# Weight decoding in a fused attention and mixture kernel: the sign bit taken on GpSimd for 18 of 32 half slices

## The chip, the cores and the metric

One core of a Trainium2 chip runs the whole program once. The metric is the device time of one execution in microseconds (us). The engines are named as the profile names them: PE (TensorE matmul) and PEld (its weight loads), DVE (VectorE), ACT (ScalarE), POOL (GpSimd), SP (SyncE, which issues most of the DMAs).

## What is computed

Three layers follow each other on 3072 tokens of 512 features.

```python
attn_out = _attn_ref(**attn_kwargs)        # chunked attention, 4 batches x 8 heads x 768 x 64, with 8 memory keys
x = attn_out.transpose(0, 2, 1, 3).reshape(B * S, H * D)
h = x @ w_in                               # 3072x512 @ 512x2048
g = h * (1.0 / (1.0 + np.exp(-h)))
x = (g @ w_out).astype(np.float32)         # 3072x2048 @ 2048x512
...                                        # then a gate, an assignment of 384 tokens to each of 8 experts,
h = np.maximum(x[mask] @ w1[e], 0.0)       # and two matmuls per expert
out[mask] = h @ w2[e]
```

`w_in` and `w_out` of the second layer arrive as 64-bit floats. The kernel has to make 32-bit floats of them on the chip, and this decoding is what the change is about.

## The kernel before

The tokens go in 8 batches of 384 (`NB`, `TB`). For each batch the second layer's hidden dimension is cut into 16 slices of 128 (`NF`). A pass of the main loop is one slice `f` of one batch `n`: `gemm1(n, f)` makes the hidden values on PE (L298), `swish` turns them into `gh` and `gl` (a tanh on ACT at L307, a product on DVE at L309, a rounded copy on ACT at L316, the rest on POOL at L317), and `gemm2` of two passes before adds its product to the accumulators (L334). Every 32-bit operand is split in a rounded part and a remainder, so that three matmuls make one exact enough product. The attention of the next batch is threaded through the passes in four items (pairs of heads): scores (`att_s`, L200 on PE, L205 on DVE, L211 on ACT), normalizing (`att_n`, L220 and L221 on DVE, L222 on POOL), transposes (`att_t`, L230 on PE, L241 on ACT) and the product with the values (`att_av`, `att_x`).

The weights of a slice are decoded once, in the opening and the passes of the first batch, and stay in SBUF. There are 32 items, one for the half of `w_in` and one for the half of `w_out` of each slice. An item is a tile `w` of 128 x 512 pairs of words (512 KB) and goes through four stages, one stage per tick:

- `w_load` (L136): SP issues the DMA. There are five buffers, so a load waits until POOL has finished with the item five before it.
- `w_bias` (L146): ACT reads the high words as floats and scales them into a PSUM bank, which moves the exponent to where a 32-bit float has it.
- `w_bits`: three DVE operations on 128 x 512 words. L152 shifts by 3, L153 ors in the upper bits of the low word, L155 ors in the sign, which it masks out of the high word.
- `w_split`: ACT rounds the result (L162), POOL subtracts the rounded part (L163).

`tick` calls the stages last first, so that one tick holds the split of item j, the bits of item j+1, the bias of item j+2 and a load. The opening is a hand-written order of steps (`PRO`, where `w0` to `w3` are the four stages; five items have their bias there). Each pass of the first batch has two ticks: `tick("a2")` ahead of `gemm1`, `tick("a1")` between `gemm1` and `gemm2`. Each engine takes its instructions in the order in which this Python code issues them; nothing reorders them later.

In the first batch `swish` is called at the end of the pass (`finish()`), so on DVE a pass reads: bits of tick a2, bits of tick a1, the product L309. On ACT it reads: the rounding copy and bias of tick a2, those of tick a1, tanh, and, as soon as DVE has L309, the copy `gh`. On POOL: the subtract of tick a2, that of tick a1, `gl`. The passes are called 0 to 15 below. The four attention items have their scores in passes 0, 3, 7 and 11, the normalizing one pass later, the transposes two passes later, the product with the values three passes later.

Of the kernel before, what the change touches and what calls it, by code (L numbers as in the profile page):

```python
# [13 lines left out]
OP = mybir.AluOpType  # L14
# [34 lines left out]
def body(ctx, tc, qk_in, v_in, wcat1, wcat2, wgt, consts, masks, iconst, bconst, out):  # L49
    nc = tc.nc  # L50
    PE, V, A, G, S = nc.tensor, nc.vector, nc.scalar, nc.gpsimd, nc.sync
# [12 lines left out]
    def bank(tag):  # L64
        return ps.tile([128, 512], F32, tag=tag, name=tag)
# [64 lines left out]
    wstage = {}  # L130
# [7 lines left out]
        wstage[i] = t  # L138

    whigh = {}  # L140

    def w_bias(i, tag):

        high = wstage[i][:, :, 1].bitcast(F32)
        whigh[i] = bank(tag)
        A.activation(out=whigh[i], in_=high, func=AF.Copy, scale=2.0 ** -112)  # L146

    def w_bits(i, tag):

        low, high = wstage[i][:, :, 0], wstage[i][:, :, 1]  # L150
        x = whigh.pop(i).bitcast(I32)
        V.tensor_scalar(out=x, in0=x, scalar1=3, scalar2=None, op0=OP.logical_shift_left)  # L152
        V.scalar_tensor_tensor(out=x, in0=low, scalar=29, in1=x,  # L153
                               op0=OP.logical_shift_right, op1=OP.bitwise_or)
        V.scalar_tensor_tensor(out=low, in0=high, scalar=-2147483648, in1=x,  # L155
                               op0=OP.bitwise_and, op1=OP.bitwise_or)
# [9 lines left out]
    def advance(k, tag="a2"):  # L166

        if stage[k] < len(items) and (k == 0 or stage[k] < stage[k - 1]):
            (w_load, w_bias, w_bits, w_split)[k](stage[k], tag)
            stage[k] += 1  # L170

    def tick(tag):
        for k in (3, 2, 1, 0):
            if k != 1 or stage[0] > stage[1] + 1 or stage[0] == len(items):
                advance(k, tag)
# [316 lines left out]
    for op in PRO.split():  # L492
        c, i, e = op[0], int(op[1]), (S, A)[op[2:] == "a"]
# [56 lines left out]
    for g in range((NB - 1) * NF):  # L550
# [8 lines left out]

        attend(0)  # L560
        tick("a2")
        finish = gemm1(n, f)
        if n > 0:
            finish()
        attend(1)
        tick("a1")
        if g >= 2:
            m, k = divmod(g - 2, NF)
# [678 lines left out]
```

## Time and profile before

| | us |
|---|---|
| median of 3 runs (lowest, highest) | 1001.63 (1001.45, 1002.49) |
| the profiled execution | 1001.23 |
| its span | 999.1 |
| PE busy | 964.9 (97%) |
| DVE busy | 682.4 (68%) |
| POOL busy | 423.3 (42%) |
| ACT busy | 404.5 (40%) |
| mean granted TensorE clock | 0.984 |

The busy shares are means over the whole span. In the 40 slices of the page PE stands at 9 tenths from the third slice on and at 7 in the first two (25 us each), while DVE has 6, 8, 8, 8, 5 in the first five. The decoding (L146 to L163) lies between 13 us and 112 us. The profiled execution lasts 1001.23 us, of which 999.1 are its span; 2.1 us lie around it.

### The profile page before, as it was taken

How to read it: one execution, taken by the hardware profiler on the slowest of the kernel's cores; microseconds unless marked ns; L12 is line 12 of the kernel's file. 1: busy time of each engine (PE TensorE's matmuls, PEld its weight loads, DVE VectorE, ACT ScalarE, POOL GpSimd, SP SyncE). 2: the span in 40 equal slices, each digit the busy share in tenths (PEclk: the TensorE clock that was granted, in tenths of full speed). 3: DMA queues.
4: the chain of work that ended last, by engine and by line, in shares of the span. 5: the costliest groups of instructions: out<-in, count | busy, mean ns of one | idle time of the engine just before them, and what ended most of it. 6: DMA issues, size and time to landing. Idle time of an engine off the chain costs nothing.

```text
span 999.1 us, 19120 instructions
## 1 busy us (share of the span) xinstructions
PE 964.9 (97%) x7193; PEld 841.0 (84%) x7193; DVE 682.4 (68%) x1958; ACT 404.5 (40%) x1000; POOL 423.3 (42%) x335
## 2 busy tenths in 40 slices
PE   7799999999999999999999999999999989999997
PEld 5687788988898888988888997778888878899996
DVE  6888578988898998898248664666766757632110
ACT  7677544343444344344343440023433333443441
POOL 3566523323232332232222441146555554767761
PEclk8799999999999999999999999999999989999999
DMA  8667321111112111111021500325444442555420
GB/s 287 214 216 231 107 81 58 39 64 41 56 64 65 32 65 60 37 64 64 33 96 45 171 1 2 127 86 189 133 143 126 129 148 85 169 169 166 151 74 31
DMA packets 34061, 102.86 MB, mean 103 GB/s; under 512 B 4145, under 2 KB 7857, under 8 KB 33970
## 3 DMA queue, kind: packets, MB, share of 16 engines
q1 hardware_dynamic: 29698, 88.63, 27.8%
q0 software_dynamic: 3840, 12.59, 3.9%
q8 instruction: 56, 0.92, 0.4%
q10 hardware_dynamic: 432, 0.43, 0.2%
q14 instruction: 35, 0.29, 0.1%
HBM read 86.69 MB, written 14.94 MB: 102 GB/s over the span
## 4 chain that ended last, share of the span: by engine, by line
PE 81%; DVE 8%; issue 3%; ACT 2%; DMA 2%; another core or an unknown queue 1%; POOL 1%; SPq 0%; POOLq 0%; DVEq 0%; ACTq 0%
PE acc L334 24%; PE h L298 23%; PE h L1045 12%; PE acc L1072 11%; PE a L772 3%; PE a L256 2%; PE a L230 2%; DVE a L153 2%; PE a L200 2%; DVE a L152 2%; DVE w L155 1%; DMA w<-in_wcat 1%; DVE junk L423 1%; PE a L971 1%
## 5 line engine op out<-in xcount | busy, mean ns | idle before, releaser
L298 PE MATMUL h<-xh,big 128*128 128x384 f32 x1024 | 289.4, 343 | 1.6 <-DVE th L309 1.6
L317 POOL TENSOR_TENSOR gl<-th,gh 128x384 fp32r<-128x384 f32 x112 | 123.3, 1101 | 253.6 <-ACT gh L316 249.7
L334 PE MATMUL acc<-big,gh 128*128 128x512 f32 x636 | 202.5, 399 | 1.2 <-ACT w L393 1.2
L298 PEld LDWEIGHTS h<-xh,big 128*128 128x128 f32 x1024 | 189.7, 190 | 9.8 <-DVE th L309 2.6
L1018 POOL TENSOR_TENSOR big<-w,big 128x1024 fp32r<-128x1024 f32 x64 | 152.4, 2394 | 71.7 <-ACT big L1017 69.1
L298 PE MATMUL h<-xl,big 128*128 128x384 f32 x512 | 174.5, 341 | 0.2 <-DVE xl L276 0.2
L334 PEld LDWEIGHTS acc<-big,gh 128*128 128x128 f32 x636 | 115.4, 189 | 21.9 <-ACT w L393 1.6
L1072 PE MATMUL acc<-big,gh 128*128 128x512 f32 x384 | 125.1, 402 | 0.0
L334 PE MATMUL acc<-big,gl 128*128 128x512 f32 x318 | 124.7, 392 | 0.0
L1045 PE MATMUL h<-xh,big 128*128 128x384 f32 x512 | 116.9, 344 | 0.7 <-ACT xh L987 0.7
L307 ACT ACTIVATE th<-h 128x384 f32<-128x384 f32 x128 | 62.3, 487 | 133.7 <-PE h L298 130.4
L423 DVE SCALAR_TENSOR_TENSOR junk<-wg_sum,w 128x512 bf16<-128x512 f32 x128 | 112.7, 880 | 3.3
L309 DVE SCALAR_TENSOR_TENSOR th<-th,h 128x384 f32<-128x384 f32 x128 | 69.8, 545 | 65.5 <-ACT th L307 65.4
L316 ACT ACTIVATE gh<-th 128x384 fp32r<-128x384 f32 x112 | 58.8, 525 | 126.5 <-DVE th L309 126.5
L298 PEld LDWEIGHTS h<-xl,big 128*128 128x128 f32 x512 | 97.6, 191 | 4.1 <-DVE xl L276 0.7
L1049 ACT ACTIVATE gh<-h 128x384 fp32r<-128x384 f32 x64 | 31.4, 491 | 160.8 <-PE h L1045 145.4
L1045 PEld LDWEIGHTS h<-xh,big 128*128 128x128 f32 x512 | 91.5, 189 | 5.8 <-ACT xh L987 0.9
L412 DVE SCALAR_TENSOR_TENSOR junk<-w 128x512 bf16<-128x512 f32 x96 | 86.2, 898 | 2.3
L1054 DVE SCALAR_TENSOR_TENSOR gl<-h,gh 128x384 fp32r<-128x384 f32 x64 | 35.4, 552 | 73.9 <-ACT gh L1049 73.8
L1072 PEld LDWEIGHTS acc<-big,gh 128*128 128x128 f32 x384 | 71.0, 190 | 8.9
L1072 PE MATMUL acc<-big,gl 128*128 128x512 f32 x192 | 77.1, 401 | 0.0
L211 ACT ACTIVATE s<-s,m 128x96 f32<-128x96 f32 x168 | 60.8, 364 | 26.8 <-DVE m L205 26.8
(216 smaller groups left out, 1446.6 us busy)
## 6 DMA issues: line engine op xcount, KB each, us to landing
w<-in_wcat SPq DMA_DIRECT2D x96, 512.0 KB, 3.8
qk<-in_qk_in SPq DMA_DIRECT2D x28, 480.0 KB, 4.4
v<-in_v_in SPq DMA_DIRECT2D x28, 288.0 KB, 3.0
x2d<-w SPq DMA_DIRECT2D x16, 256.0 KB, 2.0
w<-in_wgt SPq DMA_DIRECT2D x4, 512.0 KB, 6.4
x2d<-x SPq DMA_DIRECT2D x8, 256.0 KB, 2.1
back<-gd SPq DMA_DIRECT2D x2, 768.0 KB, 6.1
big<-in_qk_in SPq DMA_DIRECT2D x3, 480.0 KB, 7.4
```

Source lines behind the costliest of these rows:

```text
L211: A.activation(out=s[:, b, :], in_=s[:, b, :], func=AF.Exp, scale=-1.0, bias=m[:, b:b + 1], accum_out=m[:, 6 + b:7 + b])
L298: PE.matmul(b[:, :TB], w1[:, o:o + 128], (xh, xl, xh)[p][:, c, :], start=not done, stop=len(done) == 11)
L307: A.activation(out=th, in_=b[:, :TB], func=AF.Tanh, scale=0.5)
L309: V.scalar_tensor_tensor(out=u, in0=th, scalar=1.0, in1=b[:, :TB], op0=OP.add, op1=OP.mult)
L316: A.activation(out=gh, in_=u, func=AF.Copy)
L317: G.tensor_tensor(out=gl, in0=u, in1=gh.bitcast(F32), op=OP.subtract)
L334: PE.matmul(a, g[:, 128 * t:128 * t + 128], w2[:, o:o + 512], start=(f in first and p == 0), stop=(f + 1 in (*first, NF) and p == 2))
L412: V.scalar_tensor_tensor(out=junk, in0=xs[k], scalar=1.0, in1=late["w"][e], op0=OP.mult, op1=OP.mult, accum_out=Lg[:, k, e:e + 1])
L423: V.scalar_tensor_tensor(out=junk, in0=t, scalar=0.5, in1=late["w"][e], op0=OP.mult, op1=OP.mult, accum_out=part2[:, f % 4, e:e + 1])
L1018: G.tensor_tensor(out=l, in0=t, in1=h.bitcast(F32), op=OP.subtract)
L1045: PE.matmul(b[:, :TB], (h, h, l)[p][:, 128 * c:128 * c + 128], (xh, xl, xh)[p][:, c, :], start=(p == 0 and c == 0), stop=(p == 2 and c == 3))
L1072: PE.matmul(a, (gh, gh, gl)[p][:, 128 * t:128 * t + 128], (h, l, h)[p][:, 512:1024], start=(s % 8 == 0 and p == 0), stop=(s % 8 == 7 and p ...
```

## The change

For some items POOL makes the sign bit from the high words, in place, as a part of the bias stage: `(high < 0) * -2**31`, written as an integer, is the sign bit alone. The bits stage of such an item is then two DVE operations: shift the biased word and or in the sign, then or in the low word's upper bits. Which items: those whose bias is in the opening, and in the loop those whose bias is in `tick("a1")`. These are 5 and 13, 18 of 32; the other 14 keep three DVE operations.

```diff
     whigh = {}
+    part_signs = [True]
+
+
+    parted = {}
 
     def w_bias(i, tag):
 
         high = wstage[i][:, :, 1].bitcast(F32)
         whigh[i] = bank(tag)
         A.activation(out=whigh[i], in_=high, func=AF.Copy, scale=2.0 ** -112)
+        if parted.setdefault(i, part_signs[0]):
+
+            G.tensor_scalar(out=wstage[i][:, :, 1], in0=high, scalar1=0.0, scalar2=-2.0 ** 31, op0=OP.is_lt, op1=OP.mult)
 
     def w_bits(i, tag):
 
         low, high = wstage[i][:, :, 0], wstage[i][:, :, 1]
         x = whigh.pop(i).bitcast(I32)
+        if parted[i]:
+            V.scalar_tensor_tensor(out=x, in0=x, scalar=3, in1=high, op0=OP.logical_shift_left, op1=OP.bitwise_or)
+            V.scalar_tensor_tensor(out=low, in0=low, scalar=29, in1=x,
+                                   op0=OP.logical_shift_right, op1=OP.bitwise_or)
+            return
         V.tensor_scalar(out=x, in0=x, scalar1=3, scalar2=None, op0=OP.logical_shift_left)
...
     def tick(tag):
+        part_signs[0] = tag == "a1"
         for k in (3, 2, 1, 0):
```

The order of PE, ACT and SP does not change. An item whose bias is in tick a1 of a pass has its bits in tick a2 of the next pass, so in each pass the first decode on DVE is the shorter one.

On POOL, passes 3 to 5 (from `gl` of pass 3 to `gl` of pass 5; `s` is the normalizing of an attention item, the L163 rows are the splits of ticks a2 and a1). Before:

```order
L317 TENSOR_TENSOR gl<-th,gh 128x384 [waits PE_49,Activation_49]
L163 TENSOR_TENSOR big<-w,big 128x512 [waits DMAHW2_49,Activation_49]
L222 TENSOR_TENSOR s<-s,m 128x576 [waits DVE_49]
L163 TENSOR_TENSOR big<-w,big 128x512 [waits DMAHW3_49,Activation_49]
L317 TENSOR_TENSOR gl<-th,gh 128x384 [waits PE_49,Activation_49]
L163 TENSOR_TENSOR big<-w,big 128x512 [waits DMAHW4_49,Activation_49]
L163 TENSOR_TENSOR big<-w,big 128x512 [waits DMAHW5_49,Activation_49]
L317 TENSOR_TENSOR gl<-th,gh 128x384 [waits PE_49,Activation_49]
```

With the change (L153 is the sign, L175 the split, L235 the normalizing, L330 `gl`):

```order
L330 TENSOR_TENSOR gl<-th,gh 128x384 [waits PE_49,Activation_49]
L175 TENSOR_TENSOR big<-w,big 128x512 [waits DMAHW2_49,Activation_49]
L235 TENSOR_TENSOR s<-s,m 128x576 [waits DVE_49]
L175 TENSOR_TENSOR big<-w,big 128x512 [waits Activation_49]
L153 TENSOR_SCALAR w<-w 128x512 [waits DMAHW5_49,Activation_49,Pool_49]
L330 TENSOR_TENSOR gl<-th,gh 128x384 [waits PE_49,Activation_49]
L175 TENSOR_TENSOR big<-w,big 128x512 [waits DMAHW4_49,Activation_49]
L175 TENSOR_TENSOR big<-w,big 128x512 [waits Activation_49]
L153 TENSOR_SCALAR w<-w 128x512 [waits DMAHW1_49,Activation_49,Pool_49]
L330 TENSOR_TENSOR gl<-th,gh 128x384 [waits PE_49,Activation_49]
```

The sign stands behind both subtracts of its pass (and behind the normalizing where there is one) and ahead of `gl`.

On DVE, from the product of pass 3 to that of pass 4 (`th`), with the normalizing between the two decodes. Before:

```order
L309 SCALAR_TENSOR_TENSOR th<-th,h_592 128x384 [waits Activation_49]
L152 TENSOR_SCALAR a_626<-a_626 128x512
L153 SCALAR_TENSOR_TENSOR a_626<-w,a_626 128x512 [waits DMAHW3_49,DVE_49]
L155 SCALAR_TENSOR_TENSOR w<-w,a_626 128x512 [waits DVE_49,Pool_49]
L220 TENSOR_SCALAR m<-m 128x6
L221 RECIPROCAL m<-m 128x6 [waits DVE_49]
L152 TENSOR_SCALAR a_686<-a_686 128x512 [waits Activation_49]
L153 SCALAR_TENSOR_TENSOR a_686<-w,a_686 128x512 [waits DMAHW4_49,DVE_49]
L155 SCALAR_TENSOR_TENSOR w<-w,a_686 128x512 [waits DVE_49,Pool_49]
L309 SCALAR_TENSOR_TENSOR th<-th,h_690 128x384 [waits Activation_49]
```

With the change:

```order
L322 SCALAR_TENSOR_TENSOR th<-th,h_592 128x384 [waits Activation_49]
L160 SCALAR_TENSOR_TENSOR a_626<-a_626,w 128x512 [waits DMAHW3_49,Pool_49]
L161 SCALAR_TENSOR_TENSOR w<-w,a_626 128x512 [waits DVE_49]
L233 TENSOR_SCALAR m<-m 128x6
L234 RECIPROCAL m<-m 128x6 [waits DVE_49]
L164 TENSOR_SCALAR a_686<-a_686 128x512 [waits Activation_49]
L165 SCALAR_TENSOR_TENSOR a_686<-w,a_686 128x512 [waits DMAHW4_49,DVE_49]
L167 SCALAR_TENSOR_TENSOR w<-w,a_686 128x512 [waits DVE_49]
L322 SCALAR_TENSOR_TENSOR th<-th,h_690 128x384 [waits Activation_49]
```

The first decode's opening row waited for nothing new and now waits for POOL's sign; one row is gone.

On POOL at the end of the opening, with the change (before there are the four L163 rows alone):

```order
L175 TENSOR_TENSOR big<-w,big 128x512 [waits Activation_49]
L153 TENSOR_SCALAR w<-w 128x512 [waits DMAHW7_49,Activation_49]
L175 TENSOR_TENSOR big<-w,big 128x512 [waits Activation_49]
L153 TENSOR_SCALAR w<-w 128x512 [waits DMAHW1_49,Activation_49]
L175 TENSOR_TENSOR big<-w,big 128x512 [waits Activation_49]
```

These are the split of item 1, the sign of item 3, the split of item 2, the sign of item 4, the split of item 3.

## Rows read from the trace of the kernel before

**Rows 1.** Busy time by engine, 80 to 90 us (`PE, PEld, DVE, ACT, POOL`, clock, DMA share, GB/s).
```profile
80.00:90.00 10.00, 9.07 (x66) 7.64 (x67) 9.34 (x16) 7.27 (x15) 8.13 (x8) 1.00 0.58 204
```
**Rows 2.** Chain of waits, 0 to 120 us, shares by line.
```profile
by line: DVE a L153 13.0%; DVE a L152 12.5%; DVE w L155 9.7%; DMA w<-in_wcat 9.4%; issue 9.1%; DMA big<-in_qk_in 6.2%; PE h L298 5.5%; ACT s L211 4.9%; PE acc L334 4.2%; DVE th L309 2.9%; DVE m L220 2.8%; ACT a L146 2.7%; ACT big L162 2.3%;
```
**Rows 3.** Waits of PE, 28 to 110 us (us in total, times, longest).
```profile
PE a L230 <- POOL s L222: 3.4, 3, 1.6
PE a L230 <- ACT at L241: 1.9, 3, 0.8
```
**Rows 4.** The three decode operations (ns: shortest, median, longest).
```profile
L152 DVE TENSOR_SCALAR a<-a x30: 673/693/699, 14.0 to 106.3; 128x512 int32<-128x512 int32 x30
L153 DVE SCALAR_TENSOR_TENSOR a<-w,a x30: 695/697/697, 14.7 to 107.0; 128x512 int32<-128x512 int32 x30
L155 DVE SCALAR_TENSOR_TENSOR w<-w,a x30: 689/689/692, 15.4 to 107.8; 128x512 int32<-128x512 int32 x30
```
**Rows 5.** Timeline of DVE, passes 3 to 11 (start us, us, instruction).
```profile
52.24 0.55 DVE L309 SCALAR_TENSOR_TENSOR th<-th,h 128x384 f32<-128x384 f32 x1 [1.26 <-ACT th L307]
58.02 0.55 DVE L309 SCALAR_TENSOR_TENSOR th<-th,h 128x384 f32<-128x384 f32 x1
58.48 0.69 DVE L152 TENSOR_SCALAR a<-a 128x512 int32<-128x512 int32 x1
59.21 0.69 DVE L153 SCALAR_TENSOR_TENSOR a<-w,a 128x512 int32<-128x512 int32 x1
60.61 0.69 DVE L152 TENSOR_SCALAR a<-a 128x512 int32<-128x512 int32 x1
62.75 0.55 DVE L309 SCALAR_TENSOR_TENSOR th<-th,h 128x384 f32<-128x384 f32 x1
67.95 0.55 DVE L309 SCALAR_TENSOR_TENSOR th<-th,h 128x384 f32<-128x384 f32 x1
75.10 0.55 DVE L309 SCALAR_TENSOR_TENSOR th<-th,h 128x384 f32<-128x384 f32 x1 [1.27 <-ACT th L307]
97.97 0.55 DVE L309 SCALAR_TENSOR_TENSOR th<-th,h 128x384 f32<-128x384 f32 x1 [1.28 <-ACT th L307]
```
**Rows 6.** Timeline of ACT behind the product of pass 4.
```profile
58.60 0.53 ACT L316 ACTIVATE gh<-th 128x384 fp32r<-128x384 f32 x1 [2.03 <-DVE th L309]
59.03 0.65 ACT L162 ACTIVATE big<-w 128x512 fp32r<-128x512 f32 x1
59.58 0.62 ACT L146 ACTIVATE a<-w 128x512 f32<-128x512 f32 x1
```
**Rows 7.** Timeline of POOL, passes 3 to 5.
```profile
53.43 1.02 POOL L317 TENSOR_TENSOR gl<-th,gh 128x384 fp32r<-128x384 f32 x1 [4.42 <-ACT gh L316]
54.41 1.32 POOL L163 TENSOR_TENSOR big<-w,big 128x512 fp32r<-128x512 f32 x1
56.07 1.15 POOL L222 TENSOR_TENSOR s<-s,m 128x576 f32<-128x576 f32 x1 [0.34 <-DVE m L221]
57.18 1.31 POOL L163 TENSOR_TENSOR big<-w,big 128x512 fp32r<-128x512 f32 x1
60.19 2.63 POOL L163 TENSOR_TENSOR big<-w,big 128x512 fp32r<-128x512 f32 x2
```
**Rows 8.** Groups of POOL by shape (busy us, mean ns, idle before).
```profile
L163 POOL TENSOR_TENSOR big<-w,big 128x512 fp32r<-128x512 f32 x32 | 42.0, 1312 | 12.3 <-ACT big L162 12.2
L1018 POOL TENSOR_TENSOR big<-w,big 128x1024 fp32r<-128x1024 f32 x64 | 152.4, 2394 | 71.7 <-ACT big L1017 69.1 <-DVE ind L763 2.3
```
**Rows 9.** Timeline of the end of the opening: splits, bias and bits of items 1 and 4.
```profile
21.54 1.31 POOL L163 TENSOR_TENSOR big<-w,big 128x512 fp32r<-128x512 f32 x1 [2.12 <-ACT big L162]
23.80 0.64 ACT L146 ACTIVATE a<-w 128x512 f32<-128x512 f32 x1 [0.61 <-DMA w<-in_wcat]
25.63 0.69 DVE L152 TENSOR_SCALAR a<-a 128x512 int32<-128x512 int32 x1
```
**Rows 10.** Waits of ACT for loads, 0 to 120 us.
```profile
ACT a L146 <- DMA w<-in_wcat: 1.3, 2, 0.7
```

## Prediction

> **What bounds the kernel now.** I read the busy time by stretches first, to see whether one stage differs from the rest. It does: from 80 to 90 us DVE is busy 9.34 of 10 us, PE 9.07 and POOL 8.13 [rows 1], while the whole program is 97% PE. So a saving on DVE counts in the stage in which the weights are decoded and nowhere else. The chain of waits says the same: of the first 120 us, 35% lie on the three decode lines [rows 2]. The waits of PE show where it pays for that: at the transposes, which wait for POOL's normalizing and for ACT's copy of the first half [rows 3], both of which hang on DVE. Behind pass 13 PE stands at 9 tenths or more in nearly every slice of the page and has no such waits, so the gain of the whole program is how much earlier pass 13's transposes come.
>
> The timeline of DVE gives the clock of this stage: the products (L309) of passes 3 to 7 start at 52.24, 58.02, 62.75, 67.95 and 75.10 us, and that of pass 11 at 97.97 [rows 5]. So four passes, with one attention item in them, take 22.86 us, twice in a row (22.87 the second time). The single passes take 5.78, 4.73, 5.20 and 7.15.
>
> **What is removed.** One decode occupies DVE for 60.61 - 58.48 = 2.13 us; its first operation takes 59.21 - 58.48 = 0.73 of that [rows 5]. The new pair is two operations of the kind of L153 and L155, with one operand in SBUF and one in PSUM as those have, 696 and 690 ns [rows 4], so it takes the other 1.40. 18 items save 18 x 0.73 = 13.1 us of DVE time. This would be the gain if nothing else came in. Two things do.
>
> **ACT behind the first decode.** The second decode of a pass needs the bias of tick a2. After a product at t, ACT starts `gh` at t + 0.58, the rounding copy at t + 1.01, the bias at t + 1.56, and ends it at t + 2.18 [rows 6]. The short first decode would end at t + 0.46 + 1.40 = 1.86. So where DVE has nothing between the two decodes (passes 5 and 6), the second starts at about t + 2.2, and 0.4 of the 0.73 is left. Where normalizing or scores lie between (passes 4 and 7), all of it is left.
>
> **The sign on POOL, and who waits for it.** The trace has no one-input operation of this size on POOL, so its time X is bounded. From below by what an operation there costs beside its elements: the split takes 1.312 us for 512 columns and 2.394 for 1024 [rows 8], that is 2.11 ns a column and 0.23 fixed. From above by the split itself, 1.31, which streams two inputs. With one of two inputs, half of the 1.08 us for the columns is 0.77 in all; comparing and multiplying will not be quite free. I take 0.85 as an estimate, nearer to the half than to the whole.
>
> The Trainium skill (GPSIMD Engine Reference, Engine selection) says that one-input operations on this engine go at about line rate; with its 1.2 GHz that is 0.43 us of columns, 0.66 with the fixed part, an estimate that no row here shows. By it the sum below would be 4.6 us in place of 3.0.
>
> The sign is queued behind both subtracts of its pass. From `gl` of pass 3 at 53.43 POOL goes on to a subtract at 54.41 [rows 7]. The normalizing waits for DVE there; 0.73 earlier it follows the subtract at once, at 55.72, the second subtract 1.11 later at 56.83, and ends at 58.14 [rows 7]. Written from the product of pass 3 (t = 0): `gl` 1.19, sign from 5.90 to 6.75. In a pass without normalizing two subtracts take 2.63 [rows 7], and the sign ends 0.99 + 2.63 + X = 4.47 behind the start of `gl`. Behind the sign on POOL stand `gl` and the next splits, behind the waiting DVE operation the second decode and the next product. I allow 0.06 from POOL to DVE. So through one period:
>
> - Pass 4: its first decode's sign was made in pass 7's counterpart, where POOL idles. Nothing waits. Product at 5.78 - 0.73 = 5.05.
> - Pass 5: decode ready at 5.05 + 0.47 = 5.52, sign at 6.75 + 0.06 = 6.81. DVE waits 1.29. Product at 6.81 + 1.40 + 2.13 = 10.34; before it was 10.51. The gain is 0.17.
> - Pass 6: `gl` of pass 4 could start at 5.05 + 1.18 and starts behind the sign, 6.75, so the next sign ends at 11.22. Decode at 11.28 (0.47 of waiting), product, with 0.46 for an attention remainder, at 11.28 + 1.40 + 2.13 + 0.46 = 15.27; before 15.71. The gain is 0.44.
> - Pass 7: `gl` of pass 5 at 10.34 + 1.18 = 11.52, sign at 15.99, decode at 16.05 (ready at 15.74). The rest of the pass is 7.15 - 0.47 - 0.73 = 5.95, product at 22.00. The gain of the period is 22.86 - 22.00 = 0.86.
>
> So of 4 x 0.73 = 2.9 a period keeps 0.9; DVE gives most of it back in waits for a sign that arrives late.
>
> **The opening.** Its loads set the pace to the last: the bias of item 4 starts at 23.80 when its load lands, and ends at 24.44; its decode starts at 25.63 and ends at 27.76 [rows 9]. POOL's order now is split 1, sign 3, split 2, sign 4. Split 1 started at 21.54 [rows 9]; with the earlier signs ahead of it I put it at 21.8. Then 21.8 + 1.31 + 0.85 + 1.31 + 0.85 = 26.12, decode from 26.2 to 27.6. The gain is 0.15, from five items.
>
> **The sum.** Opening 0.15; passes 1 to 3 repeat passes 4 to 6, 0.44; two periods (passes 4 to 11), 1.72; pass 12 repeats pass 4, 0.73, and releases the transposes of pass 13. Together 3.04 us. I cost at nothing: the later `gl` (its product in `gemm2` is two passes away, some 10 us), and the loads, which wait for the splits: ACT waited for a load only twice, 1.3 us, both times in the opening [rows 10]. If the splits came a tick later, loads would be late next. The profiled execution of 1001.23 (span 999.1, 2.1 around it) would go to 998.2; the median of the runs is 0.40 above that execution, so the forecast for a median is **998.6**.
>
> The same steps with X at its ends: at 0.23 the waits all but vanish, the period is 20.9, the opening gives 1.0, and the sum is 7.0, 994.6. At 1.31 the period is 23.1, the opening loses 1.2, the passes 1 to 3 lose 0.5, and the sum is -1.4, 1003.0. Each 0.1 us of X costs about 0.75 us, and the gain is nil at X of 1.15.
>
> **Rivals.**
> 1. *POOL sets the pace* (slower). If the sign takes as long as the split or longer, POOL has 1.0 + 2.63 + X to do in each pass of 4.73 and, through `gl`, passes its lateness on. The place is the first decode of passes 5 to 7 and those like them; it decides from X = 1.15, and is outside the noise of 2 us from about 1.4. At 1.4 the time is 1003.7. For it: POOL is already busy 81% here [rows 1], every row of it is slower per column than DVE's, and the sign has two steps per element. Against: it reads one tensor, not two. The Trainium skill (GPSIMD Engine Reference, its opening paragraphs) calls this engine the wrong choice for ordinary elementwise work, VectorE being about 2 times faster; twice the 0.69 us of the removed operation is 1.38. The splits here agree with that ratio in kind; whether a one-input operation does no row shows.
> 2. *It cancels* (the same). X is between about 1.0 and 1.4, the decode is shorter by what it waits longer: 1000 to 1003, most likely 1001.
> 3. *The sign is cheap* (much faster). X below 0.65, DVE sets the pace again and ACT's bias is next: 994.6 to 997.
> 4. *The change does not do what it says*: DVE is not what binds this stage, since PE is 91% busy in it. Then an early decode would only end in PE's queue. Against that stand PE's waits at the transposes, 2.4 us in a period [rows 3], as much as the largest gain asks for. I give it no number of its own but count it in the second.
>
> PE's granted clock is another unknown: it falls in parts of the opening and the first passes, behind waits of PE, and these waits will change by some tenths. I allow 1 us to either side.
>
> **How the numbers follow.** 0.2% is 2.0 us, about what a measurement of this kernel can tell from no change. X between 0.65 and 0.98, the forecast: 0.44. Below 0.65: 0.10. Together faster, 0.54. Rival 2 with rival 4: 0.28. Rival 1 beyond 2 us: 0.18. The range leaves out the lowest part of the cheap cases and a part of rival 1: 995.4 to 1003.2. The forecast's own case spans 997.0 to 999.6.
>
> **What would show it.** POOL's new row (TENSOR_SCALAR, 128x512, 18 times): 0.65 to 0.98 us, else the sum moves by 0.75 for each 0.1. DVE's new first operation has waits ended by POOL, longest in passes 5, 9 and 13, about 1.3 us each, none in passes 4, 8 and 12. Products a period apart by 22.0 in place of 22.86. Decoding ends about 3 us earlier, the opening's share of it nearly nothing. It would be wrong in its mechanism if DVE did not wait for POOL and the period still stayed above 22, or if ACT began to wait for loads in the loop.

## The result, and the profile after

The change makes the kernel slower. Its median is 1011.01 us (6 runs, 1008.43 to 1013.0) against 1002.06 for the kernel before in the same runs; the ratio is 1.0092, with a 95% interval of 1.0076 to 1.0108. Forecast was 998.6, range 995.4 to 1003.2.

The new row on POOL, from the groups by shape (busy us, mean ns, idle before), beside the split, which did not change ([rows 8]):

```profile
L175 POOL TENSOR_TENSOR big<-w,big 128x512 fp32r<-128x512 f32 x32 | 42.0, 1313 | 6.5 <-ACT big L174 6.5
L153 POOL TENSOR_SCALAR w<-w 128x512 int32<-128x512 f32 x18 | 35.9, 1992 | 1.0 <-ACT a L150 1.0
```

The sign takes 1.99 us, more than the split with its two inputs. The prediction had allowed 0.23 to 1.31.

What DVE waits for, 0 to 122 us (us in total, times, longest), the first two rows:

```profile
DVE a L160 <- POOL w L153: 22.3, 15, 2.9
DVE th L322 <- ACT th L320: 5.1, 4, 1.3
```

With the two opening items whose bank lies in another tile (1.5 us) DVE waits 23.8 us for the sign. Before, no decode waited for POOL. The pair saves 18 x 0.73 = 13.1 us of DVE time, so DVE is 10.7 us worse off, near the 9 us that the span grew (999.1 to 1008.1). The two need not be equal, since 7.0 us of the waits lie in the opening and a part of what the pair saves there was never on the path.

The products on DVE, passes 3 to 7 and pass 11, which answer to [rows 5]:

```profile
58.30 0.55 DVE L322 SCALAR_TENSOR_TENSOR th<-th,h 128x384 f32<-128x384 f32 x1 [1.27 <-ACT th L320]
62.73 0.55 DVE L322 SCALAR_TENSOR_TENSOR th<-th,h 128x384 f32<-128x384 f32 x1
66.15 0.70 DVE L160 SCALAR_TENSOR_TENSOR a<-a,w 128x512 int32<-128x512 int32 x1 [2.88 <-POOL w L153]
69.63 0.56 DVE L322 SCALAR_TENSOR_TENSOR th<-th,h 128x384 f32<-128x384 f32 x1
71.68 0.70 DVE L160 SCALAR_TENSOR_TENSOR a<-a,w 128x512 int32<-128x512 int32 x1 [1.50 <-POOL w L153]
75.55 0.54 DVE L322 SCALAR_TENSOR_TENSOR th<-th,h 128x384 f32<-128x384 f32 x1
77.17 0.70 DVE L160 SCALAR_TENSOR_TENSOR a<-a,w 128x512 int32<-128x512 int32 x1 [1.08 <-POOL w L153]
83.00 0.55 DVE L322 SCALAR_TENSOR_TENSOR th<-th,h 128x384 f32<-128x384 f32 x1 [1.27 <-ACT th L320]
108.07 0.55 DVE L322 SCALAR_TENSOR_TENSOR th<-th,h 128x384 f32<-128x384 f32 x1 [1.27 <-ACT th L320]
```

A period of four passes takes 24.70 us, then 25.07; before it was 22.86. The first decode of passes 5, 6 and 7 waits 2.88, 1.50 and 1.08 us for the sign, that of pass 4 not at all. POOL in the same stretch, which answers to [rows 7]:

```profile
59.49 1.02 POOL L330 TENSOR_TENSOR gl<-th,gh 128x384 fp32r<-128x384 f32 x1 [2.61 <-ACT gh L329]
60.47 1.33 POOL L175 TENSOR_TENSOR big<-w,big 128x512 fp32r<-128x512 f32 x1
61.74 1.16 POOL L235 TENSOR_TENSOR s<-s,m 128x576 f32<-128x576 f32 x1
62.85 1.32 POOL L175 TENSOR_TENSOR big<-w,big 128x512 fp32r<-128x512 f32 x1
64.13 1.99 POOL L153 TENSOR_SCALAR w<-w 128x512 int32<-128x512 f32 x1
66.06 1.04 POOL L330 TENSOR_TENSOR gl<-th,gh 128x384 fp32r<-128x384 f32 x1
67.03 2.65 POOL L175 TENSOR_TENSOR big<-w,big 128x512 fp32r<-128x512 f32 x2
69.64 2.01 POOL L153 TENSOR_SCALAR w<-w 128x512 int32<-128x512 f32 x1
```

The row order is the one that was read before the run: the sign stands behind the splits, DVE's decode starts 0.03 us behind its end, and `gl` starts only then. Busy time from 90 to 100 us (PE, PEld, DVE, ACT, POOL), which answers to [rows 1]:

```profile
90.00:100.00 10.00, 8.47 (x63) 7.00 (x61) 7.07 (x11) 6.67 (x14) 10.00 (x8) 1.00 0.51 161
```

POOL is busy without a gap in this stretch, DVE has fallen from 9.34 to 7.07. Over the whole period of passes 8 to 11 POOL is busy 23.23 of 25.07 us (15.55 of 22.87 before) and DVE 18.38 (20.45 before). In the chain of waits from 0 to 122 us the sign has the largest share, 23.3%, where the three decode operations had it before [rows 2]. The bound of the stage has moved from DVE to POOL, though not to POOL's work alone: each period has a gap on POOL of some 1.3 us, in front of the second split of its last pass:

```profile
80.65 1.33 POOL L175 TENSOR_TENSOR big<-w,big 128x512 fp32r<-128x512 f32 x1 [1.27 <-ACT big L174]
```

That split waits for ACT's rounding, which stands in ACT's queue behind the attention item; the item waits for its scores on DVE, and these stand behind the first decode, which had waited 1.08 us for the sign. A gap of this size was there before the change too, when POOL had time to spare.

### The profile page after: what moved, and what is told of

Read it like the earlier page. It is cut to its first block, busy times and chain, and to the rows that moved or that the text cites. A ratio compares the mean times of both kernels' runs of the same rounds, so it can differ in the third digit from the quotient of the medians.

```text
span 1008.1 us, 19096 instructions
## 1 busy us (share of the span) xinstructions
PE 964.1 (96%) x7193; PEld 839.7 (83%) x7193; DVE 671.6 (67%) x1940; ACT 404.0 (40%) x1000; POOL 458.3 (45%) x353
## 4 chain that ended last, share of the span: by engine, by line
PE 82%; POOL 5%; DVE 4%; issue 3%; ACT 3%; another core or an unknown queue 1%; DMA 0%; POOLq 0%
PE acc L347 24%; PE h L311 23%; PE h L1058 13%; PE acc L1085 11%; POOL w L153 3%; PE a L785 3%; PE a L269 2%; PE a L213 2%; PE a L243 2%; POOL big L175 1%; DVE junk L436 1%; PE a L984 1%; ACT s L224 1%; DVE a L160 1%
## 5 line engine op out<-in xcount | busy, mean ns | idle before, releaser
L330 POOL TENSOR_TENSOR gl<-th,gh 128x384 fp32r<-128x384 f32 x112 | 124.5, 1111 | 233.8 <-ACT gh L329 229.9
L235 POOL TENSOR_TENSOR s<-s,m 128x576 f32<-128x576 f32 x28 | 33.1, 1183 | 86.6 <-DVE m L234 86.6
```

What stands on the lines that cost most here:

```text
L330: G.tensor_tensor(out=gl, in0=u, in1=gh.bitcast(F32), op=OP.subtract)
```

## The experiments

Two questions were open: whether the sign's time alone makes the loss (the late-sign theory) or something else that the change brought with it (the pair on DVE, the queue place, the waits as such), and why the sign takes 1.99 us. Each run is compared with the kernel before on its own chip; that one's median was 998.69 us for the first four runs, 989.20 for the next four and 989.78 for the last three, so ratios and differences are compared, not times. "Pass 15" is the start of the last product of the first batch in the profile, behind which PE paces everything; it is at 119.93 us before and at 129.96 with the change. From there to the end the profiled executions (without the two rows of added operations) take 877 to 879 us before, with the change and in the first group of runs, and 866 to 868 us in the other two groups. So that is where the chips differ, and starts ahead of it can be set side by side across chips. They carry an offset, though: the first bias of the decoding starts anywhere between 12.88 and 13.71 us, in kernels that do the same up to there (12.99 before).

### The opening alone

```diff
     def tick(tag):
-        part_signs[0] = tag == "a1"
+        part_signs[0] = False
```

> The sign on POOL for the 5 items of the opening alone; the loop decodes with three DVE operations as before. Late-sign theory (the sign takes 1.99 us in POOL's queue and DVE waits for it): the product of pass 0 starts near 36.5 us as in the changed kernel (32.5 before), and from there the periods are 22.9 us as before: about 4 us slower than before. Rival, that the loss is one of the loop alone (POOL full there) and the opening has idle time to hide in: within 1 us of before.

Measured: ratio 1.0057 (1.0038 to 1.0077), 6.0 us slower in the median. The product of pass 0 starts at 36.41 us, and pass 15 is at 123.46, 3.5 us later than before. The periods are 22.90 and 22.87 us. So the five items of the opening lose by themselves, as the late-sign theory said; the rival falls. The median lost more than the 3.5 to 4 us that the trace shows; its interval (3.8 to 7.7 us) reaches down to it.

### The loop alone

```diff
-    part_signs = [True]
+    part_signs = [False]
```

> The sign on POOL for the 13 items of the loop alone; the opening as before. Late-sign theory: product of pass 0 at 32.5 us, periods of four passes 24.7 to 25.1 us in place of 22.9, DVE waits for POOL about 1.4 to 2.9 us in three passes of four: about 5 us slower than before. Rival, that the opening's delay alone costs the time: within 1 us of before.

Measured: ratio 1.0073 (1.0048 to 1.0098), 7.7 us slower. Pass 0 at 33.29, periods of 24.72 and 25.08 us, pass 15 at 126.58, 6.7 us later than before. The two parts add up in the trace: 3.5 + 6.7 = 10.2, and with both it is 10.0. The medians do not add up so well, 6.0 + 7.7 = 13.7 against 9.0 for both on another chip, but their intervals (3.8 to 7.7, 4.8 to 9.8 and 7.6 to 10.8 us) allow it.

### The pair on DVE without the sign

The sign operation is left out; DVE ors in the raw high words.

```diff
-            G.tensor_scalar(out=wstage[i][:, :, 1], in0=high, scalar1=0.0, scalar2=-2.0 ** 31, op0=OP.is_lt, op1=OP.mult)
+            pass
```

> The two DVE operations for the 18 items, reading the high words as they are; the sign operation on POOL is left out, so the weights of these items have other values. Late-sign theory: without the wait DVE keeps what the pair saves, less the 0.3 us that ACT's bias takes back in two passes of four: periods of 20.5 to 21 us, about 6 to 8 us faster than before. Rival, that DVE does not bind this stage (PE does): no faster than before by over 2 us. Second rival, that the pair itself is slow or collides with POOL: slower than before.

Measured: ratio 0.9922 (0.9902 to 0.9942), 6.6 us faster than before. Products of passes 3 to 7 on DVE:

```profile
49.90 0.56 DVE L322 SCALAR_TENSOR_TENSOR th<-th,h 128x384 f32<-128x384 f32 x1 [1.27 <-ACT th L320]
54.41 0.55 DVE L322 SCALAR_TENSOR_TENSOR th<-th,h 128x384 f32<-128x384 f32 x1
56.64 0.70 DVE L164 TENSOR_SCALAR a<-a 128x512 int32<-128x512 int32 x1 [0.29 <-ACT a L150]
58.93 0.55 DVE L322 SCALAR_TENSOR_TENSOR th<-th,h 128x384 f32<-128x384 f32 x1
64.04 0.54 DVE L322 SCALAR_TENSOR_TENSOR th<-th,h 128x384 f32<-128x384 f32 x1
70.45 0.56 DVE L322 SCALAR_TENSOR_TENSOR th<-th,h 128x384 f32<-128x384 f32 x1 [1.27 <-ACT th L320]
```

The periods are 20.55 and 21.30 us; in the second ACT waits 1.36 us for a load. DVE did bind this stage, and in pass 5 the second decode waits for ACT's bias, 2.23 us behind the product. Both rivals fall. Passes 4 to 7 take 1.27, 0.21, 0.09 and 0.74 us less than before; 0.54 of the 1.27 is not the pair's but that of a normalizing operation which became shorter (last section). PE is now busy 20.42 of the 20.55 us, so by this row little more can be had in such a period.

Pass 0 starts at 32.49, as before, which looks as if the opening gained nothing. But in this trace the first bias starts at 13.71 us in place of 12.99, so from there to pass 0 it takes 18.78 us in place of 19.50, and 19.3 to 20.4 in the three other traces with an unchanged opening. So the opening does gain some 0.7 us without a sign.

### What the sign costs by itself, first row of operations

The kernel before, with POOL operations on a scratch tile behind the last matmul, when the other engines are idle. `hi` is every second word, `flat` is contiguous, `hint` and `fint` are the same as integers.

```diff
...
+    for _ in range(2):
+        G.tensor_scalar(out=hint, in0=hi, **two)                   # L1164: compare, multiply
+        G.tensor_scalar(out=hi, in0=hi, **two)                     # L1165: float output
+        G.tensor_scalar(out=hi, in0=hi, **arith)                   # L1166: multiply, add
+        G.tensor_scalar(out=hi, in0=hi, **lt)                      # L1167: compare alone
+        G.tensor_scalar(out=hi, in0=hi, **one)                     # L1168: multiply alone
+        G.tensor_scalar(out=flat, in0=flat, **two)                 # L1169
+        G.tensor_scalar(out=flat, in0=flat, **one)                 # L1170
+        G.tensor_scalar(out=hint[:, 0:256], in0=hi[:, 0:256], **two)   # L1171
...
```

> The kernel before with a row of POOL operations behind its last matmul, on a scratch tile, each twice (so some 30 us longer): the sign as in the change, the same with a float output, two arithmetic steps, a compare alone, a multiply alone, both on contiguous words, half the columns, a two-input product. If 1.99 us is paid per step: the one-step forms take about 1.1. If it is paid for the integer output: the float output takes 1.3 or less. If for the stride of two words: the contiguous forms take about 1. If DVE's work beside it delayed the sign: the sign here takes under 1.5 us. Half the columns tell the fixed part: 1.1 if it is 0.23 us.

Groups of POOL by shape (busy us, mean ns, idle before):

```profile
L1164 POOL TENSOR_SCALAR w<-w 128x512 int32<-128x512 f32 x2 | 4.0, 1986 | 0.1
L1165 POOL TENSOR_SCALAR w<-w 128x512 f32<-128x512 f32 x2 | 3.9, 1962 | 0.2
L1166 POOL TENSOR_SCALAR w<-w 128x512 f32<-128x512 f32 x2 | 1.3, 638 | 0.2
L1167 POOL TENSOR_SCALAR w<-w 128x512 f32<-128x512 f32 x2 | 3.1, 1534 | 0.2
L1168 POOL TENSOR_SCALAR w<-w 128x512 f32<-128x512 f32 x2 | 3.1, 1536 | 0.2
L1169 POOL TENSOR_SCALAR w<-w 128x512 f32<-128x512 f32 x2 | 3.9, 1930 | 0.2
L1171 POOL TENSOR_SCALAR w<-w 128x256 int32<-128x256 f32 x2 | 2.2, 1098 | 0.2
L1173 POOL TENSOR_TENSOR w<-w 128x512 f32<-128x512 f32 x2 | 2.1, 1038 | 0.2
```

The sign takes 1.99 us with nothing beside it, so DVE's work is not the cause. Neither is the integer output (1.96 without) nor the stride (1.93 without). Half the columns take 1.10, so a column costs 3.47 ns and the fixed part is 0.21. A single step takes 1.53, not half. A product of two inputs (L1173, behind the cut of the edit) takes 1.04, less than the multiply of one input by a constant, 1.54 (L1168). And the odd one: multiplying and adding, two steps as well, takes 0.64. None of the four explanations was right; which pair of steps it is decides. Why POOL prices them so, no run shows.

### Which pairs are quick, second row of operations

The same kernel with other operations behind the last matmul.

```diff
...
+        form(hi, hi, 0.0, OP.mult, -0.0, OP.add)
+        form(hi[:, 0:256], hi[:, 0:256], 0.0, OP.mult, -0.0, OP.add)
+        form(hint, hi, 0.5, OP.mult, 1.0, OP.add)
+        form(hi, hi, 0.5, OP.mult, 2.0, OP.mult)
+        form(hi, hi, 1.0, OP.add, 2.0, OP.mult)
+        form(hi, hi, 0.5, OP.max, 2.0, OP.min)
+        form(hi, hi, 0.0, OP.is_lt, 1.0, OP.add)
+        form(hi, hi, 1.0, OP.add)
...
```

> The kernel before with a second row of POOL operations behind its last matmul, 128 x 512, stride of two words, each twice. If multiplying and adding is a routine of its own: multiply by 0.0 and add -0.0 takes 0.64 us (256 columns: 0.43), with integer output little more, and all other pairs (two multiplies, add and multiply, maximum and minimum, compare and add) 1.9 to 2.0, a lone add 1.5. If any pair without a compare is fast: those too take 0.64.

All of these share a line, so each is shown by its own stretch of the timeline: one row of each, in the order of the edit (busy us, mean ns, idle before).

```profile
L1160 POOL TENSOR_SCALAR w<-w 128x512 f32<-128x512 f32 x1 | 0.6, 647 | 0.0
L1160 POOL TENSOR_SCALAR w<-w 128x256 f32<-128x256 f32 x1 | 0.4, 414 | 0.1
L1160 POOL TENSOR_SCALAR w<-w 128x512 int32<-128x512 f32 x1 | 0.6, 639 | 0.1
L1160 POOL TENSOR_SCALAR w<-w 128x512 f32<-128x512 f32 x1 | 0.6, 639 | 0.1
L1160 POOL TENSOR_SCALAR w<-w 128x512 f32<-128x512 f32 x1 | 0.6, 638 | 0.1
L1160 POOL TENSOR_SCALAR w<-w 128x512 f32<-128x512 f32 x1 | 2.0, 1971 | 0.1
L1160 POOL TENSOR_SCALAR w<-w 128x512 f32<-128x512 f32 x1 | 2.0, 1977 | 0.1
L1160 POOL TENSOR_SCALAR w<-w 128x512 f32<-128x512 f32 x1 | 1.5, 1543 | 0.1
```

The expectation was too narrow: not one pair but all three pairs of multiplies and adds take 0.64 us. Pairs with a compare, a maximum or a minimum take 1.97, and a lone add 1.54, more than twice a pair of the quick kind. A column of the quick kind costs 0.91 ns.

### The sign as a multiply and an add

A negative number times 0.0 is -0.0, whose only set bit is the sign; adding -0.0 leaves both zeros as they are. So the sign can be had from the quick pair, in the same place.

```diff
-            G.tensor_scalar(out=wstage[i][:, :, 1], in0=high, scalar1=0.0, scalar2=-2.0 ** 31, op0=OP.is_lt, op1=OP.mult)
+            G.tensor_scalar(out=high, in0=high, scalar1=0.0, scalar2=-0.0, op0=OP.mult, op1=OP.add)
```

> The change with one line altered: the sign is made as high times 0.0 plus -0.0, which leaves the sign bit alone and is the multiply-and-add pair that took 0.64 us in the row of POOL operations, in place of the compare and multiply of 1.99 us. Same queue places, same DVE work, same waits. Late-sign theory: the sign's length alone decides; with 0.64 the prediction's own steps give about 4 us faster than before (3 to 6), DVE waits for POOL under 0.5 us a pass. Rival, that any POOL operation at this place costs the waits (queue place, semaphores): slower than before by 2 us or more.

Measured: ratio 0.9930 (0.9914 to 0.9947), 6.5 us faster than before. The sign stands in the same place of POOL's queue with the same waits and only its length differs, and the loss becomes a gain. The rows of the sign and of what DVE waited for, 0 to 125 us:

```profile
L153 POOL TENSOR_SCALAR w<-w x18: 637/655/671, 13.8 to 98.8; 128x512 f32<-128x512 f32 x18
DVE a L160 <- POOL w L153: 7.3, 8, 1.6
```

The waits fall from 23.8 to 7.8 us (0.5 of it in the other bank), the periods to 21.24 and 21.84. Run again beside the next version it gave 0.9934 (0.9920 to 0.9947), as expected:

> The fast sign for all 18 items behind the split, as in the fast-sign run, again, beside the run with the sign ahead: ratio to the kernel before 0.992 to 0.995.

### The quick sign in the loop alone

On the version with the quick sign:

```diff
-    part_signs = [True]
+    part_signs = [False]
```

> The same fast sign, in the loop alone (13 items), the opening as before. If the opening gains nothing from the pair (the run without any sign began pass 0 at 32.49 us, as before) and only pays for POOL's extra operations, this is as fast as the one with all 18 or up to 1 us faster: 4 to 5 us faster than before. If the opening does gain with a short sign, it is slower than that one by up to 1 us.

Measured: ratio 0.9944 (0.9928 to 0.9961), 5.9 us faster than before; pass 15 at 114.32, with all 18 items at 113.60. The two intervals overlap, so the times do not tell what the opening's five items do with a quick sign. The traces do: from the first bias to pass 0 it takes 19.27 us here and 18.50 to 18.53 in the three runs with a quick sign in the opening, so it gains about 0.8 us there. The expectation's premise, that the opening gains nothing, was wrong.

### The quick sign in both ticks of the loop

```diff
-        part_signs[0] = tag == "a1"
+        part_signs[0] = True
```

> The fast sign in both ticks of every pass of the loop (all 27 items of the loop), the opening as before. DVE then spends 1.4 us less in a pass than before, POOL 1.28 us more: 1.0 + 2.63 + 1.28 = 4.9 us a pass and 1.1 more where it normalizes, so POOL sets the pace at 20.7 us for four passes. Late-sign theory: within 2 us of the run with 13 items, DVE waiting for POOL again. Rival, that DVE is all that counts: 4 us faster still.

Measured: ratio 1.0038 (1.0024 to 1.0052), 4.2 us slower than before. Both expectations fail. DVE waits 27.3 us for the sign, and the period is 24.67 us, far above what POOL's work adds up to. Pass 5 of POOL with the start of pass 6, products of DVE at 58.41 and 64.30, and DVE's second decode of pass 5:

```profile
60.00 1.02 POOL L330 TENSOR_TENSOR gl<-th,gh 128x384 fp32r<-128x384 f32 x1
60.99 1.30 POOL L175 TENSOR_TENSOR big<-w,big 128x512 fp32r<-128x512 f32 x1
62.27 0.65 POOL L153 TENSOR_SCALAR w<-w 128x512 f32<-128x512 f32 x1
65.48 1.02 POOL L330 TENSOR_TENSOR gl<-th,gh 128x384 fp32r<-128x384 f32 x1 [0.64 <-ACT gh L329]
```

```profile
62.96 0.70 DVE L160 SCALAR_TENSOR_TENSOR a<-a,w 128x512 int32<-128x512 int32 x1 [1.46 <-POOL w L153]
```

An item whose bias is in tick a2 has its bits in tick a1 of the same pass. So the sign of a pass stands behind `gl` of the pass before, `gl` behind the product, and the next product behind that sign: 1.18 + 0.99 + 1.29 + 0.65 + 0.04 + 1.34 = 5.5 us at least in every pass. The passes take 5.48, 5.89, 5.94 and 7.36 us; on top of the loop come 0.41 in pass 5, where `gl` starts that much later behind another sign, 0.47 in pass 6 for an attention operation on DVE, and 1.9 in pass 7 for the scores and a wait for the tanh. POOL is idle before the last `gl` shown, so it is this loop and not POOL's work that binds. With the sign in tick a1 alone that loop spans two passes.

### The sign ahead of the split

```diff
...
         for k in (3, 2, 1, 0):
+            if k == 0:
+                subtract()
             if k != 1 or stage[0] > stage[1] + 1 or stage[0] == len(items):
                 advance(k, tag)
```

`w_split` only notes its subtract, and `subtract()` issues it on POOL behind the bias stage. First with the quick sign:

> The fast sign for all 18 items, and in a tick POOL gets the sign ahead of the split's subtract in place of behind it. Late-sign theory: the sign ends 1.31 us earlier, so DVE's waits for it (7.8 us in the fast-sign run, 1.55 the longest, behind the normalizing) fall under 2.5 us in all, and ACT's bias is the next limit: 1 to 2 us faster than the fast-sign run, about 8 us faster than before. Rival, that the splits, later by 0.65 us, hold up loads or PE: no faster than the fast-sign run.

Measured: ratio 0.9922 (0.9908 to 0.9935), 8.3 us faster than before, 1.8 us faster in the median than the quick sign behind the split on the same chip, though the two intervals overlap. DVE's wait for the sign and ACT's for loads, 0 to 125 us:

```profile
DVE a L160 <- POOL w L153: 1.9, 6, 0.4
ACT a L150 <- DMA w<-in_wcat: 3.2, 5, 1.2
```

DVE hardly waits for POOL any more, and ACT begins to wait for loads. Pass 15 is at 112.03 us, as early as without any sign (112.48). PE is busy 20.66 of the 20.79 us of passes 4 to 7. This is the fastest version by its median.

Then with the slow sign of the change:

> The change as it is (sign of 1.99 us), with the sign ahead of the split's subtract in the loop's ticks. If the place in POOL's queue made the loss, the loop's part of it goes: DVE's waits in the loop (17 us) fall under 5, and about 4 us slower than before are left, from the opening. If POOL's time as such makes it (1.0 + 2.63 + 1.99 = 5.6 us a pass, 23.6 for four passes with a normalizing), the period stays at 23.6 to 24 and it is 5 to 7 us slower than before.

Measured: ratio 1.0053 (1.0038 to 1.0068), 5.0 us slower than before. Busy time from 80 to 90 us:

```profile
80.00:90.00 10.00, 8.55 (x46) 7.42 (x45) 7.92 (x14) 6.77 (x14) 10.00 (x9) 1.00 0.60 202
```

The periods are 23.37 and 23.64 us, and in the second POOL is busy 23.07 us, so with 1.99 us it is now POOL's work as such that binds: 5.6 us a pass and 1.1 for the normalizing. The queue place costs the rest of the change's 24.70 to 25.07, and that is the larger part. From pass 0 (36.27 us) to pass 15 (124.78) it takes 88.51 us, with the change 93.49 and before 87.44. So of the 6.1 us that the loop had lost, about 5 went with the order of POOL's queue; most of what this version still loses comes from the opening, where pass 0 starts 3.8 us later than before. Neither expectation holds as it stood: DVE still waits 12.7 us for the sign in the loop (16.8 with the change), yet the loop loses only 1.1 us.

## Why the prediction was wrong

**The step that failed** is the bound on X: "From above by the split itself, 1.31, which streams two inputs." The number of inputs is not what bounds a one-input operation: in the first row of operations a multiply of two inputs takes 1.04 us, a multiply of one by a constant 1.54, and a compare and multiply of one 1.99. The sign measured 1.99 us, above the upper end, and since the estimate of 0.85 and the range were built between them, the forecast and the range fell with it.

**The mechanism held.** The prediction's chain, fed with 1.99 in place of 0.85, puts the sign of pass 4 at 5.90 + 1.99 = 7.89 behind the product of pass 3, the decode of pass 5 at 7.95, its product at 11.48, and those of passes 6 and 7 at 17.55 and 25.12. The trace has 11.33, 17.25 and 24.70. One of its steps is 0.6 us off: the product of pass 4, worked out at 5.05, came at 4.43, since the normalizing on DVE was shorter (last section). The places were right too: no wait in pass 4, the longest in passes 5, 9 and 13 (2.88, 1.97 and 1.96 us; pass 2 has 1.97 too). Only there were waits in passes 8 and 12 as well, 0.42 and 0.39 us, since POOL came late out of the period before.

**The rival that came true** is the first, POOL setting the pace, in the place that it named. It had 0.18. The rate of 0.75 us for each 0.1 us of sign gives 1003.0 + 0.68 x 7.5 = 1008.1 at 1.99, that is 6.5 us slower; measured was 9.0 slower (1011.0). Its point of no gain, 1.15 us, was not run; a straight line between the two lengths that were, 0.65 us (6.5 faster) and 1.99 (9.0 slower), crosses at about 1.2, an estimate. The Trainium skill's rule beside it (GPSIMD Engine Reference, its opening paragraphs: about twice VectorE's time) would have made the sign 1.38; the direction agrees, the trace has 1.99 against the 0.69 of the removed shift, a ratio of 2.9, though these are two different operations. The Trainium skill's other rule (GPSIMD Engine Reference, Engine selection: one-input operations at about line rate) disagrees with the change's operation at 3.47 ns a column and agrees with the quick pairs, at 0.91 ns.

**The saving on DVE** was right in kind: with the sign out of the way the period is 20.55 us, where the prediction had 20.9 for the shortest sign, and ACT's bias is next, 2.23 us behind the product (2.2 predicted). That the figures lie so close is in part luck: passes 5 and 6 kept 0.21 and 0.09 us of the pair's 0.73 where 0.4 each was worked out, and the normalizing gave 0.54 that nobody had counted; without it the period would be about 21.1, an estimate. With a sign of 0.65 us the kernel gained 6.5 us where the prediction's figure for 0.66 was 4.6. The normalizing's operation is 0.47 us shorter there in each of four passes, 1.9 us in all, which can account for the difference.

**The opening** came out near its working at both ends, with the sign's length again as what was off. It was given 1.0 us of gain at the shortest sign, and from the first bias to pass 0 the runs gain 0.7 without a sign and 1.0 with a quick one (18.78 and 18.50 to 18.53 us, against 19.50). It was given 0.15 of gain at 0.85 us and a loss of 1.2 at 1.31; the straight line through these gives a loss of 3.2 at 1.99, and measured from the first bias it lost 3.4 (22.86).

**PE's clock**, for which the prediction allowed 1 us, did move. Its mean over passes 0 to 3, as granted, was 0.76 of full speed before, 0.81 with the change and 0.90 to 0.91 in the versions with no sign or a quick one. With the sign in the opening alone it was 0.87, DVE had the same work in these passes as before, and they took 19.29 us in place of 19.75. So up to some 0.5 us of the gains above may be the clock's, an estimate from these two traces.

That loads would be late next if the decode sped up was right at the end: ACT waits 3.2 us for them in the fastest version, all of it in the loop; before, 1.3 [rows 10], all in the opening. PE's waits at the transposes, which the prediction saw as the place where the gain would be had, fell in it to 1.3 us behind POOL, from 3.4 [rows 3]. But they are not the whole place. The 2.4 us that the prediction counts in a period are those of passes 8 to 11; in passes 4 to 7 PE waited there for 0.36 us, and that period shortened as well.

## What to carry to other kernels

An operation that no row of the trace shows has no upper bound from its neighbours: run it once by itself before moving work to it, and try other ways of writing the same value, since here two spellings of one sign bit differ threefold in time and turn a loss of 9 us into a gain of 6.5. When work goes to an engine that is idle on average, lay its queue out in order and ask which instruction of the busy engine comes to stand behind which of its instructions; then try the new one ahead of what nobody waits for (with the slow sign that alone took back 5 of the 6 us which the loop had lost). A loop through several engines can bind by its length while none of them is fully loaded. And before two traces are compared by the start of some operation, look whether they were level at the start of the stage.

## What the hardware showed

On POOL, of the operations with scalars that were run, only the pairs of multiplies and adds were quick: 0.64 us for 128 x 512, against 1.96 to 1.99 for pairs with a compare, maximum or minimum, and 1.54 for a lone multiply, add or compare. The multiply by 0.0 takes 1.54 us alone and 0.65 with an add of -0.0 behind it, which changes nothing in the result. Stride (8 bytes) and output type change 0.05 us at most.

The normalizing's first operation on DVE, 128 x 6 elements, takes 0.17 us by its median but 0.92 in pass 4 before the change, and ends with the subtract that POOL is at. Before, and with the change:

```profile
54.85 0.92 DVE L220 TENSOR_SCALAR m<-m 128x6 f32<-128x6 f32 x1
```

```profile
60.10 0.44 DVE L233 TENSOR_SCALAR m<-m 128x6 f32<-128x6 f32 x1
85.31 1.21 DVE L233 TENSOR_SCALAR m<-m 128x6 f32<-128x6 f32 x1
```

54.85 + 0.92 is 55.77, and POOL's subtract that began at 54.41 ends at 55.73 [rows 7]; 60.10 + 0.44 is 60.54, and `gl` above ends at 60.51; 85.31 + 1.21 is 86.52, and the split that began at 85.17 ends at 86.49. The same holds to 0.04 us in all four items of the first batch, before and with the change. So it waits for POOL's instruction to be over, without a semaphore, and the profile counts that as busy time. The Trainium skill (SBUF — State Buffer, Who interferes with whom) says that a VectorE operation of this kind can take a pair of SBUF ports that GpSimd shares, and that the later one then blocks fully; these rows agree. How long it is depends on how far POOL is in its instruction. In pass 4 of the change, and in all such passes of the versions with no sign or a quick one (0.37 to 0.45 us), it was about 0.5 us shorter than before, which is most of why pass 4 took 4.43 us and 4.51, where 5.05 was worked out. In passes 1, 8 and 12 of the change it was longer than before, 1.11 to 1.25 us.
